# Nine tokens on a partition: a new layout of q, k, V and of the result in a threshold-attention and maxout kernel

## The chip, the cores and the metric

The kernel runs on one core of a Trainium2 chip. Time is device time in microseconds (us) of one execution. An execution that is over 1.5% above the fastest of the same kernel counts as slow. Ratios leave these out; the medians quoted include them. Engines: PE multiplies matrices, DVE reduces and does elementwise work, ACT evaluates activations, POOL does elementwise work, and SP's queue issues transfers. Sixteen DMA engines carry the transfers.

Ratios are the mean time of one kernel's fast runs over that of the other's fast runs of the same rounds, with a 95% interval, so they are not quite the ratio of the medians quoted beside them.

## The reference

Attention over 8 batches of 8 heads, 576 tokens and head size 64, in which only scores within tau of the row's maximum count, followed by a feed-forward layer that takes the maximum of three products:

```python
scores = scale * q @ k^T
scores = where(scores >= max(scores) - tau, scores, -1e9)
attn = softmax(scores)
x = (attn @ v), heads side by side        # 4608 x 512
h = max(x @ w1, x @ w2, x @ w3)           # 4608 x 768
out = h @ w_out                           # 4608 x 512
```

## The kernel before

Four heads of a batch make a "quad". A quad has nine steps of 128 queries for two heads; beside each step PE does two pieces of other work: transposes of the next quad's q and k (`tp`), products of the probabilities with V (`o`), hidden pieces of the feed-forward (`ph`), blocks of its output (`po`). In the profile's lines `sc` are scores, `P` the probabilities, `ptq` the transposed probabilities, and `ob` a block of the result that ACT copies out of PSUM and a store takes away. All PSUM results share four buffers. The probabilities are transposed by the DMA engines (`ptq<-P`), issued from the same SP queue as the loads and stores. The parts that the change touches, cut:

```python
# load: four tokens on a partition, the last 64 tokens apart
nc.sync.dma_start(out=L[n + "m"][:, hh],
                  in_=src[b, hs, 0:512, :].rearrange("h (p c) d -> p h c d", c=4))
nc.sync.dma_start(out=L[n + "r"][:, hh], in_=src[b, hs, 512:S, :].rearrange("h p d -> p h d"))
...
# transposed: four full transposes and a half one, five a head pair and tensor
for src in (m[:, h1, 0:2], m[:, h1, 2:4], r[:, h0:h0 + 2], m[:, h0, 0:2], m[:, h0, 2:4]):
    np_ = src.shape[0]
    tensor.transpose(ps[:, col:col + np_], src.rearrange("p a d -> p (a d)"), identf[:np_, :np_])
...
# product: the fifth block of keys has 64 rows
rows = slice(0, 64) if i == 1 else slice(64, 128)
w = vrb[rows, pr, :]
x = pt[rows, 4, q0:q0 + n]
...
# outp: 128 rows of the result, or the last 64
rows = out[b * S:b * S + 512, :].rearrange("(p c) m -> c p m", c=4)[c] if c < 4 \
    else out[b * S + 512:(b + 1) * S, :]
nc.sync.dma_start(out=rows, in_=ob[:r])
```

Of the kernel before, what the change touches and what calls it, by code (L numbers as in the profile page):

```python
# [11 lines left out]
F32 = mybir.dt.float32  # L12
# [34 lines left out]
def kernel(  # L47
# [19 lines left out]

    nc = tc.nc
# [30 lines left out]
    qk = ctx.enter_context(tc.tile_pool(name="qk", bufs=4))  # L99
# [12 lines left out]
    def load(b, qd, split=False):  # L112
        h = slice(4 * qd, 4 * qd + 4)
        L = dict(b=b, qd=qd)
        for n in "qk":
            L[n + "m"] = ld.tile([128, 4, 4, D], F32, name=n + "m")
            L[n + "r"] = ld.tile([64, 4, D], F32, name=n + "r")
        for hh in ((slice(0, 2), slice(2, 4)) if split else (slice(0, 4),)):
            for n, src in (("q", q), ("k", k)):
                hs = slice(4 * qd + hh.start, 4 * qd + hh.stop)  # L120
                nc.sync.dma_start(out=L[n + "m"][:, hh],
                                  in_=src[b, hs, 0:512, :].rearrange("h (p c) d -> p h c d", c=4))
                nc.sync.dma_start(out=L[n + "r"][:, hh], in_=src[b, hs, 512:S, :].rearrange("h p d -> p h d"))
        vm = ld.tile([128, 4, 4, D], F32, name="vm")
        vr = ld.tile([128, 2, D], F32, name="vr")
        nc.sync.dma_start(out=vm, in_=v[b, h, 0:512, :].rearrange("h (p c) d -> p h c d", c=4))
        rest = v[b, h, 512:S, :].rearrange("(t i) p d -> i p t d", i=2)
        nc.sync.dma_start(out=vr[0:64], in_=rest[1])
        nc.sync.dma_start(out=vr[64:128], in_=rest[0])
        L["vm"], L["vr"] = vm, vr  # L130
        return L

    def cast_v(L):
        vb = vp.tile([128, 4, 4, D], BF16, name="vb")
        vrb = vp.tile([128, 2, D], BF16, name="vrb")
        pool.tensor_copy(out=vb, in_=L["vm"])
        pool.tensor_copy(out=vrb, in_=L["vr"])
        L["vb"], L["vrb"] = vb, vrb

    def transposed(L, n, pr):  # L140

        m, r = L[n + "m"], L[n + "r"]
        ps = slot("tp")
        h0, h1 = 2 * pr, 2 * pr + 1
        col = 192
        for src in (m[:, h1, 0:2], m[:, h1, 2:4], r[:, h0:h0 + 2], m[:, h0, 0:2], m[:, h0, 2:4]):
            np_ = src.shape[0]
            tensor.transpose(ps[:, col:col + np_], src.rearrange("p a d -> p (a d)"), identf[:np_, :np_])
            col += np_
        t = qk.tile([128, S], F32, name=n + "t")  # L150
        if n == "q":
            scalar.activation(out=t, in_=ps[:, 192:768], func=AF.Copy, scale=scale)
            s = qk.tile([128, S], F32, name="qs")
            pool.tensor_copy(out=s[0:64], in_=t[64:128])
            pool.tensor_copy(out=s[64:128], in_=t[0:64])
            L["qs", pr] = s
        else:
            vector.tensor_copy(out=t, in_=ps[:, 192:768])
        L[n + "t", pr] = t


    def scores(L, idx, i):

        ps = slot("sc")
        first = 256 if i == 1 else 192
        for r in range(2):
            cols = slice(first, 512) if r == 0 else slice(512, first + S)
            if i == 1:
                kc = slice(0, 256) if r == 0 else slice(0, 320)
            else:  # L170
                kc = slice(256, 576) if r == 0 else slice(320, 576)
# [14 lines left out]
    def masked(idx, i):  # L186
        return i == 0 and idx in MASKED

    def maximum(idx, i, sc):
# [3 lines left out]
        if masked(idx, i):  # L193
            return nm
# [251 lines left out]
```

## Time and profile before

| | before |
|---|---|
| time, median | 542.63 us (541.65 to 543.3) |
| steady stage, one batch | 62.45 us, PE busy 61.2, DVE 50.9, ACT 50.3 |
| score pieces, first start | 9.43 us |
| time of SP's packets, as a share of the span of 16 DMA engines | 72.9% |

The prediction shows the page's main rows. Two more matter in hindsight: the transfers' totals, and the profile's account of the transposing transfers (durations of the issue in ns, lowest, median and highest; then the time from issue to landing).

```profile
DMA packets 220086, 84.06 MB, mean 156 GB/s; under 512 B 185472, under 2 KB 215424, under 8 KB 220032
q1 hardware_dynamic: 214464, 80.24, 72.9%
...
L224 SPq DMA_TRANSPOSE ptq<-P x144: 1242/1308/7147, 18.9 to 512.5; - x144
...
DMA to landing us min/median/max: 3.2/3.5/15.3
```

The packets of SP's queue take nearly three quarters of what 16 engines have, without being what bounds the kernel: DMA is 3% of the end-setting chain. A transposing transfer is issued in 1.3 us and lands after 3.5. The 72.9% is a mean over 16 engines: it leaves room if the work stays spread evenly over them.

### The profile page before, as it was taken

How to read it: one execution, taken by the hardware profiler on the slowest of the kernel's cores; microseconds unless marked ns; L12 is line 12 of the kernel's file. 1: busy time of each engine (PE TensorE's matmuls, PEld its weight loads, DVE VectorE, ACT ScalarE, POOL GpSimd, SP SyncE). 2: the span in 40 equal slices, each digit the busy share in tenths (PEclk: the TensorE clock that was granted, in tenths of full speed). 3: DMA queues.
4: the chain of work that ended last, by engine and by line, in shares of the span. 5: the costliest groups of instructions: out<-in, count | busy, mean ns of one | idle time of the engine just before them, and what ended most of it. 6: DMA issues, size and time to landing. Idle time of an engine off the chain costs nothing.

```text
span 537.3 us, 10760 instructions
## 1 busy us (share of the span) xinstructions
PE 502.1 (93%) x3638; PEld 305.5 (57%) x3652; DVE 412.4 (77%) x988; ACT 405.0 (75%) x819; POOL 292.1 (54%) x402
## 2 busy tenths in 40 slices
PE   7779759999999999999999999999999999899996
PEld 4335336565566645665566655666566665566563
DVE  2998956887598868887699867888688896587542
ACT  3998966687877878788787878878877878686732
POOL 3688984554554745565465545647455665342310
PEclk9999887999999999999999999999999999899999
DMA  7999999996976678879866587966879446543461
GB/s 212 234 240 199 207 154 180 222 189 140 201 177 126 144 190 138 178 127 190 188 154 130 127 208 167 191 130 147 191 135 173 89 90 143 100 88 70 132 106 49
DMA packets 220086, 84.06 MB, mean 156 GB/s; under 512 B 185472, under 2 KB 215424, under 8 KB 220032
## 3 DMA queue, kind: packets, MB, share of 16 engines
q1 hardware_dynamic: 214464, 80.24, 72.9%
q0 software_dynamic: 5568, 3.15, 5.0%
q8 instruction: 28, 0.46, 0.4%
q14 instruction: 26, 0.21, 0.1%
HBM read 34.60 MB, written 9.44 MB: 82 GB/s over the span
## 4 chain that ended last, share of the span: by engine, by line
PE 68%; DVE 13%; ACT 4%; DMA 3%; issue 1%; POOL 0%; ACTq 0%; DVEq 0%
PE sc L35 23%; PE ph L35 22%; PE po L35 9%; PE o L35 8%; DVE nm L35 6%; PE tp L35 6%; DMA ptq<-P 3%; ACT z L35 3%; DVE hm L35 2%; DVE z L35 1%; DVE hT L35 1%; DVE bm L35 1%; ACT xt L35 1%; ACT hm L35 0%; DVE xt L35 0%
## 5 line engine op out<-in xcount | busy, mean ns | idle before, releaser
L35 POOL TENSOR_SCALAR P<-z,rs 128x576 bf16<-128x576 f32 x288 | 214.1, 756 | 209.8 <-ACT z L35 179.3
L35 DVE TENSOR_REDUCE nm<-sc 128x1 f32<-128x576 f32 x288 | 215.8, 750 | 54.1 <-PE sc L35 54.0
L35 ACT ACTIVATE z<-sc,bm 128x576 f32<-128x576 f32 x192 | 141.9, 741 | 87.6 <-DVE bm L35 66.0
L35 PE MATMUL sc<-kt,qs 64*128 64x320 f32 (+2 forms) x640 | 186.9, 435 | 6.7 <-ACT z L35 6.0
L35 PE MATMUL sc<-kt,qt 64*128 64x256 f32 (+2 forms) x640 | 185.5, 445 | 3.6 <-ACT z L35 3.5
L35 PE MATMUL ph<-xt,w 128*128 128x288 bf16 (+2 forms) x1152 | 157.2, 289 | 3.4 <-ACT xt L35 2.6
L35 PEld LDWEIGHTS <-w 128*128 128x128 bf16 x1152 | 107.3, 98 | 55.9 <-issue 28.9
L35 ACT ACTIVATE z<-z 128x576 f32<-128x576 f32 x192 | 130.4, 683 | 0.0
L35 PEld LDWEIGHTS sc<-kt,qs 64*128 64x128 f32 (+1 forms) x640 | 91.6, 178 | 40.5 <-ACT z L35 28.1
L35 PEld LDWEIGHTS sc<-kt,qt 64*128 64x128 f32 (+1 forms) x640 | 92.2, 178 | 25.0 <-ACT z L35 10.3
L35 DVE SCALAR_TENSOR_TENSOR z<-z 128x576 f32<-128x576 f32 x96 | 76.0, 792 | 0.0
L35 ACT ACTIVATE z<-sc,nm 128x576 f32<-128x576 f32 x96 | 70.9, 739 | 0.0
L35 PE MATMUL po<-wo,hT 128*128 128x512 bf16 (+1 forms) x226 | 56.4, 381 | 2.2 <-DVE hT L35 1.5
L35 POOL COPY qs<-qt 64x576 f32<-64x576 f32 x64 | 48.9, 764 | 9.6 <-ACT qt L35 6.2
L35 DVE TENSOR_TENSOR hm<-ph,hm 128x576 bf16<-128x576 f32 (+2 forms) x54 | 36.9, 682 | 22.4 <-PE ph L35 9.2
L35 PE MATMUL o<-ptq,vb 128*64 128x288 bf16 (+3 forms) x528 | 44.4, 290 | 8.8 <-DMA ptq<-P 6.5
L35 ACT ACTIVATE hm<-ph 128x576 bf16<-128x576 f32 (+2 forms) x54 | 32.2, 595 | 15.0 <-PE ph L35 14.3
L35 PEld LDWEIGHTS <-hT 128*128 128x128 bf16 (+1 forms) x240 | 22.2, 100 | 31.4 <-issue 7.0
L35 DVE TENSOR_TENSOR hT<-ph,hm 128x576 bf16<-128x576 f32 (+2 forms) x54 | 36.9, 683 | 3.8 <-PE ph L35 1.2
L35 PEld LDWEIGHTS <-vb 128*64 128x64 bf16 x528 | 24.4, 109 | 25.9 <-issue 15.6
L35 ACT ACTIVATION_READ_ACCUMULATOR z<-z 128x1 f32 x192 | 38.6, 201 | 0.0
L35 PE MATMUL tp<-identf,qm 128*128 128x128 f32 x128 | 28.9, 309 | 6.3 <-DMA qm<-in_q_dram 3.6
(28 smaller groups left out, 296.7 us busy)
## 6 DMA issues: line engine op xcount, KB each, us to landing
vm<-in_v_dram SPq DMA_DIRECT2D x16, 512.0 KB, 4.9
out_dram<-ob SPq DMA_DIRECT2D x32, 256.0 KB, 2.6
qm<-in_q_dram SPq DMA_DIRECT2D x15, 512.0 KB, 4.4
km<-in_k_dram SPq DMA_DIRECT2D x15, 512.0 KB, 5.0
ptq<-P SPq DMA_TRANSPOSE x144, 3.5
w<-in_moe_w_dram POOLq DMA_DIRECT2D x9, 256.0 KB, 9.1
vr<-in_v_dram SPq DMA_DIRECT2D x32, 32.0 KB, 4.1
out_dram<-ob SPq DMA_DIRECT2D x8, 128.0 KB, 2.8
```

Source lines behind the costliest of these rows:

```text
L35: ins = fn(*a, **kw)
```

## The change

The intent: with nine tokens of a head on each of 64 partitions, and two heads on 128, all transposes are full ones, runs in HBM grow to 2304 bytes, V's last keys need no 64-row matmuls, and the last tokens of the result use both halves of the array's columns. The core of the diff, cut:

```diff
+        def part(src, r, i=None):
+            h = slice(4 * qd + r, 4 * qd + 4, 2) if i is None else slice(4 * qd + r + 2 * i, 4 * qd + r + 2 * i + 1)
+            return src[b, h].rearrange("i (p c) d -> i p c d", c=9)
+
+        for i in ((0, 1) if first else (None,)):
+            rows = slice(0, 128) if i is None else slice(64 * i, 64 * i + 64)
+            q2 = nc.scalar if first else nc.sync
+            nc.sync.dma_start(out=L["q"][rows, 0:9], in_=part(q, 0, i))
+            q2.dma_start(out=L["k"][rows, 0:9], in_=part(k, 0, i))
 ...
+        nj = 5 - r
+        for j in range(nj):
+            tensor.transpose(ps[:, 128 * j:128 * j + 128], couple(L, n, r, j),
+                             identf)
 ...
+                for r in range(2):
+                    x = pt[:, 4 if m == 4 else m + 5 * r, q0:q0 + n]
 ...
+            rows = out[b * S:(b + 1) * S, :].rearrange("(p c) m -> c p m", c=9)
+            if c < 4:
 ...
+                rows = rows[first:first + 5:4]
 ...
+                    for x in range(2):
+                        tensor.matmul(ps[64 * x:64 * x + 64, :256], hT[:, f, 512:S], wo[:, f, 256 * x:256 * x + 256],
+                                      start=(f == 0), stop=(f == NF - 1))
 ...
+                rows = rows[8].rearrange("p (x m) -> x p m", x=2)
 ...
-    for a in prep:
-        transposed(Ls[0], *a)
+    for a in prep[:1] + prep[1:2]:
+        transposed_one(Ls[0], a[0], 0)
```

`transposed_one` does the first quad's transposes for one head pair at a time with 64 rows, so that the first scores need not wait for the other pair.

More of the change, by code (lines that the diff above doesn't have):

```diff
@@ L98 @@
     vp = ctx.enter_context(tc.tile_pool(name="vp", bufs=3))
-    qk = ctx.enter_context(tc.tile_pool(name="qk", bufs=4))
+    qk = ctx.enter_context(tc.tile_pool(name="qk", bufs=2))
     zz = ctx.enter_context(tc.tile_pool(name="zz", bufs=4))
@@ L109, in slot @@
         return ps_s.tile([128, 1024], F32, name=name, tag="s")
-    def load(b, qd, split=False):
-        h = slice(4 * qd, 4 * qd + 4)
-        L = dict(b=b, qd=qd)
-        for n in "qk":
-            L[n + "m"] = ld.tile([128, 4, 4, D], F32, name=n + "m")
-            L[n + "r"] = ld.tile([64, 4, D], F32, name=n + "r")
-        for hh in ((slice(0, 2), slice(2, 4)) if split else (slice(0, 4),)):
-            for n, src in (("q", q), ("k", k)):
-                hs = slice(4 * qd + hh.start, 4 * qd + hh.stop)
-                nc.sync.dma_start(out=L[n + "m"][:, hh],
-                                  in_=src[b, hs, 0:512, :].rearrange("h (p c) d -> p h c d", c=4))
-                nc.sync.dma_start(out=L[n + "r"][:, hh], in_=src[b, hs, 512:S, :].rearrange("h p d -> p h d"))
-        vm = ld.tile([128, 4, 4, D], F32, name="vm")
-        vr = ld.tile([128, 2, D], F32, name="vr")
-        nc.sync.dma_start(out=vm, in_=v[b, h, 0:512, :].rearrange("h (p c) d -> p h c d", c=4))
-        rest = v[b, h, 512:S, :].rearrange("(t i) p d -> i p t d", i=2)
-        nc.sync.dma_start(out=vr[0:64], in_=rest[1])
-        nc.sync.dma_start(out=vr[64:128], in_=rest[0])
-        L["vm"], L["vr"] = vm, vr
@@ new lines, with load @@
+    FIRST = dict(q=((0, 4, 2, 6), (10, 14, 12, 16)), k=((4, 0, 6, 2), (14, 10, 16, 12)))
+    vms = [one.tile([128, 4, 5, D], F32, name=f"vm{x}") for x in range(2)]
+    def load(g, first=False):
+        b, qd = quads[g]
+        L = dict(b=b, qd=qd, vm=vms[g % 2])
+        for n in "qk":
+            L[n] = ld.tile([128, 18, D], F32, name=n + "m")
+        def part(src, r, i=None):
[6 more added lines that the diff above has]
+            q2.dma_start(out=L["k"][rows, 0:9], in_=part(k, 0, i))
+            nc.sync.dma_start(out=L["q"][rows, 10:18], in_=part(q, 1, i)[:, :, 0:8])
+            nc.sync.dma_start(out=L["q"][rows, 9:10], in_=part(q, 1, i)[:, :, 8:9])
+            q2.dma_start(out=L["k"][rows, 9:18], in_=part(k, 1, i))
+        for r in range(2):
+            src = part(v, r).rearrange("i p c d -> p i c d")
+            for half, c0, c1, at_ in (((0, 4, 9, 0), (1, 0, 4, 0)), ((0, 5, 9, 1), (1, 0, 5, 0)))[r]:
+                nc.sync.dma_start(out=L["vm"][64 * half:64 * half + 64, 2 * r:2 * r + 2, at_:at_ + c1 - c0, :],
+                                  in_=src[:, :, c0:c1, :])
@@ L131, in load @@
         return L
     def cast_v(L):
-        vb = vp.tile([128, 4, 4, D], BF16, name="vb")
-        vrb = vp.tile([128, 2, D], BF16, name="vrb")
+        vb = vp.tile([128, 4, 5, D], BF16, name="vb")
         pool.tensor_copy(out=vb, in_=L["vm"])
-        pool.tensor_copy(out=vrb, in_=L["vr"])
-        L["vb"], L["vrb"] = vb, vrb
-    def transposed(L, n, pr):
-        m, r = L[n + "m"], L[n + "r"]
-        ps = slot("tp")
-        h0, h1 = 2 * pr, 2 * pr + 1
-        col = 192
-        for src in (m[:, h1, 0:2], m[:, h1, 2:4], r[:, h0:h0 + 2], m[:, h0, 0:2], m[:, h0, 2:4]):
-            np_ = src.shape[0]
-            tensor.transpose(ps[:, col:col + np_], src.rearrange("p a d -> p (a d)"), identf[:np_, :np_])
-            col += np_
-        t = qk.tile([128, S], F32, name=n + "t")
-        if n == "q":
-            scalar.activation(out=t, in_=ps[:, 192:768], func=AF.Copy, scale=scale)
-            s = qk.tile([128, S], F32, name="qs")
-            pool.tensor_copy(out=s[0:64], in_=t[64:128])
-            pool.tensor_copy(out=s[64:128], in_=t[0:64])
-            L["qs", pr] = s
-        else:
-            vector.tensor_copy(out=t, in_=ps[:, 192:768])
-        L[n + "t", pr] = t
@@ L162, in scores, with couple @@
-    def scores(L, idx, i):
-        ps = slot("sc")
-        first = 256 if i == 1 else 192
-        for r in range(2):
-            cols = slice(first, 512) if r == 0 else slice(512, first + S)
-            if i == 1:
-                kc = slice(0, 256) if r == 0 else slice(0, 320)
-            else:
-                kc = slice(256, 576) if r == 0 else slice(320, 576)
-            rows = slice(64 * r, 64 * r + 64)
+        L["vb"] = vb
+    def couple(L, n, r, j, rows=slice(0, 128)):
+        f = 8 if j == 4 else FIRST[n][r][j]
+        return L[n][rows, f:f + 2, :].rearrange("p a d -> p (a d)")
@@ new lines, in evacuated, with targets @@
+    def evacuated(L, n, dst, src):
+        if n == "q":
+            scalar.activation(out=dst(L["qt"]), in_=src, func=AF.Copy, scale=scale)
+            for x in range(2):
+                pool.tensor_copy(out=dst(L["qs"])[64 * x:64 * x + 64], in_=dst(L["qt"])[64 - 64 * x:128 - 64 * x])
+        else:
+            vector.tensor_copy(out=dst(L["kt"]), in_=src)
+    def targets(L, n):
+        if n + "t" not in L:
+            L[n + "t"] = qk.tile([128, 2, S], F32, name=n + "t")
+            if n == "q":
+                L["qs"] = qk.tile([128, 2, S], F32, name="qs")
@@ new lines, in transposed, with transposed_one @@
+    def transposed(L, n, r):
+        targets(L, n)
+        ps = slot("tp")
+        nj = 5 - r
+        for j in range(nj):
+            tensor.transpose(ps[:, 128 * j:128 * j + 128], couple(L, n, r, j),
+                             identf)
+        off = 320 * r
+        evacuated(L, n, lambda t: t[:, :, off:off + 64 * nj].rearrange("p i (j u) -> p i j u", u=64),
+                  ps[:, 0:128 * nj].rearrange("p (j i u) -> p i j u", i=2, u=64))
+    def transposed_one(L, n, i):
+        targets(L, n)
+        ps = slot("tp")
+        rows = slice(64 * i, 64 * i + 64)
+        col = 256
+        for r, j in [(0, j) for j in range(5)] + [(1, j) for j in range(4)]:
+            tensor.transpose(ps[:, col:col + 64], couple(L, n, r, j, rows),
+                             identf[rows, rows])
+            col += 64
+        evacuated(L, n, lambda t: t[:, i, :], ps[:, 256:256 + S])
@@ L173, in scores @@
+    def scores(L, idx, r):
+        ps = slot("sc")
+        first = 256 if r == 0 else 192
+        for x in (1, 0):
+            cols = slice(first, 512) if x == 1 else slice(512, first + S)
+            if r == 0:
+                kc = slice(0, 256) if x == 1 else slice(0, 320)
+            else:
+                kc = slice(256, 576) if x == 1 else slice(320, 576)
+            rows = slice(64 * x, 64 * x + 64)
             if idx != 4:
-                pr, c = (0, idx) if idx < 4 else (1, idx - 5)
@@ L175, in scores @@
-                t = L["qt", pr] if c % 2 == r else L["qs", pr]
-                off = (0 if i == 1 else 320) + 128 * (c // 2)
-                tensor.matmul(ps[:, cols], t[rows, off:off + 128], L["kt", pr][rows, kc],
+                i, c = (0, idx) if idx < 4 else (1, idx - 5)
+                t = L["qt"] if c // 2 == x else L["qs"]
+                off = 320 * r + 128 * (c % 2)
+                tensor.matmul(ps[:, cols], t[rows, i, off:off + 128], L["kt"][rows, i, kc],
                               start=True, stop=True)
@@ L179, in scores @@
             else:
-                for pr in range(2):
-                    t = L["qt", pr] if i == r else L["qs", pr]
-                    tensor.matmul(ps[64 * pr:64 * pr + 64, cols], t[rows, 256:320],
-                                  L["kt", pr][rows, kc], start=True, stop=True)
+                for i in range(2):
+                    t = L["qt"] if r == x else L["qs"]
+                    tensor.matmul(ps[64 * i:64 * i + 64, cols], t[rows, i, 256:320],
+                                  L["kt"][rows, i, kc], start=True, stop=True)
@@ L184, in scores, with masked, maximum @@
         return ps[:, first:first + S]
-    def masked(idx, i):
-        return i == 0 and idx in MASKED
-    def maximum(idx, i, sc):
+    def masked(idx, r):
+        return r == 1 and idx in MASKED
+    def maximum(idx, r, sc):
         nm = small.tile([128, 1], F32, name="nm")
         vector.tensor_reduce(out=nm, in_=sc, axis=AX, op=OP.max, negate=True)
-        if masked(idx, i):
+        if masked(idx, r):
             return nm
@@ L197, in maximum, with exponents @@
         return bm
-    def exponents(idx, i, z, sc, bias):
-        zn = z[:, (1 - i) * S:(2 - i) * S]
-        if masked(idx, i):
+    def exponents(idx, r, z, sc, bias):
+        zn = z[:, r * S:(r + 1) * S]
+        if masked(idx, r):
             scalar.activation(out=zn, in_=sc, func=AF.Exp, bias=bias)
@@ L205, in exponents, with numerators @@
             scalar.activation(out=zn, in_=sc, func=AF.Prelu, bias=bias, alpha=-STEEP)
-    def numerators(L, idx, i, z, sm):
-        n = 1 - i
-        zn = z[:, n * S:(n + 1) * S]
-        acc = sm[:, n:n + 1]
-        if masked(idx, i):
+    def numerators(L, idx, r, z, sm):
+        zn = z[:, r * S:(r + 1) * S]
+        acc = sm[:, r:r + 1]
+        if masked(idx, r):
             vector.scalar_tensor_tensor(out=zn, in0=zn, scalar=thr, in1=zn,
@@ L224, in normalized, with product @@
         nc.sync.dma_start_transpose(out=L["pt"][:, :, idx * 128:(idx + 1) * 128], in_=P)
-    def product(L, pr, xt, part=None):
+    def product(L, i, xt, part=None):
         ps = slot("o")
-        pt, vb, vrb = L["pt"], L["vb"], L["vrb"]
+        pt, vb = L["pt"], L["vb"]
         if part is None:
-            q0, p0 = (0, 224) if pr == 0 else (S, 192)
+            q0, p0 = (0, 224) if i == 0 else (S, 192)
             runs = ((q0, p0, 512 - p0), (q0 + 512 - p0, 512, S - 512 + p0))
         elif part == 1:
-            runs = ((0 if pr == 0 else S + 64, 0, 256),)
+            runs = ((0 if i == 0 else S + 64, 0, 256),)
         else:
-            runs = ((256, 0, 320),) if pr == 0 else ((S + 320, 0, 256), (S, 512, 64))
+            runs = ((256, 0, 320),) if i == 0 else ((S + 320, 0, 256), (S, 512, 64))
         for q0, p0, n in runs:
             for m in range(5):
-                for i in (1, 0):
-                    h = 2 * pr + i
-                    if m < 4:
-                        w = vb[:, h, (0, 2, 1, 3)[m], :]
-                        x = pt[:, (m if i == 1 else 5 + m), q0:q0 + n]
-                    else:
-                        rows = slice(0, 64) if i == 1 else slice(64, 128)
-                        w = vrb[rows, pr, :]
-                        x = pt[rows, 4, q0:q0 + n]
-                    tensor.matmul(ps[64 * i:64 * i + 64, p0:p0 + n], w, x, start=(m == 0), stop=(m == 4))
-        dst = xt[:, 2 * L["qd"] + pr, :]
-        if part is None and pr == 0:
+                for r in range(2):
+                    x = pt[:, 4 if m == 4 else m + 5 * r, q0:q0 + n]
+                    tensor.matmul(ps[64 * r:64 * r + 64, p0:p0 + n], vb[:, 2 * r + i, ((1, 3, 0, 2, 4), (2, 4, 1, 3, 0))[r][m], :], x,
+                                  start=(m == 0), stop=(m == 4))
+        dst = xt[:, 2 * L["qd"] + i, :]
+        if part is None and i == 0:
             vector.tensor_copy(out=dst, in_=ps[:, 224:224 + S])
@@ L257, in product @@
             scalar.activation(out=dst[:, 0:256], in_=ps[:, 0:256], func=AF.Copy)
-        elif pr == 0:
+        elif i == 0:
             vector.tensor_copy(out=dst[:, 256:S], in_=ps[:, 0:320])
@@ L288, in outp @@
         def outp(c):
-            r = 128 if c < 4 else 64
             ps = slot("po")
-            for f in range(NF):
-                tensor.matmul(ps[:r, :512], hT[:, f, c * 128:c * 128 + r], wo[:, f, :],
-                              start=(f == 0), stop=(f == NF - 1))
-            ob = hp_.tile([128, DM], F32, name="ob", bufs=3)
-            scalar.activation(out=ob[:r], in_=ps[:r, :512], func=AF.Copy)
-            rows = out[b * S:b * S + 512, :].rearrange("(p c) m -> c p m", c=4)[c] if c < 4 \
-                else out[b * S + 512:(b + 1) * S, :]
-            nc.sync.dma_start(out=rows, in_=ob[:r])
+            rows = out[b * S:(b + 1) * S, :].rearrange("(p c) m -> c p m", c=9)
+            if c < 4:
+                for f in range(NF):
+                    tensor.matmul(ps[:, :512], hT[:, f, c * 128:c * 128 + 128], wo[:, f, :],
+                                  start=(f == 0), stop=(f == NF - 1))
+                ob = hp_.tile([128, DM], F32, name="ob", bufs=3)
+                first = (0, 2, 1, 3)[c]
+                rows = rows[first:first + 5:4]
+                scalar.activation(out=ob, in_=ps[:, :512], func=AF.Copy)
+            else:
+                for f in range(NF):
+                    for x in range(2):
+                        tensor.matmul(ps[64 * x:64 * x + 64, :256], hT[:, f, 512:S], wo[:, f, 256 * x:256 * x + 256],
+                                      start=(f == 0), stop=(f == NF - 1))
+                ob = hp_.tile([128, DM // 2], F32, name="obr", bufs=2)
+                rows = rows[8].rearrange("p (x m) -> x p m", x=2)
+                scalar.activation(out=ob, in_=ps[:, :256], func=AF.Copy)
+            nc.sync.dma_start(out=rows, in_=ob)
         return ([lambda f=f, wi=wi: hid(f, wi) for f in range(NF) for wi in range(3)]
@@ L314, with o_step @@
     todo = []
-    def o_step(g, pr, part=None):
+    def o_step(g, i, part=None):
         b = quads[g][0]
@@ L319, in o_step @@
             xts[b] = xp.tile([128, 4, S], BF16, name="xt")
-        product(Ls[g], pr, xts[b], part)
-        if pr == 1 and quads[g][1] == 1:
+        product(Ls[g], i, xts[b], part)
+        if i == 1 and quads[g][1] == 1:
             if b not in hTs:
@@ L344 @@
         at(18 * g + 18 + (15 if early else 8), lambda g=g: o_step(g, 1))
+    at(0, lambda: transposed_one(Ls[0], "q", 1))
+    at(1, lambda: transposed_one(Ls[0], "k", 1))
     e = 18 * y
@@ L361 @@
     wl = list(weight_loads())
-    Ls[0] = load(*quads[0], split=True)
-    for a in prep:
-        transposed(Ls[0], *a)
-    sc = [scores(Ls[0], 0, 1), scores(Ls[0], 0, 0)]
+    for x in range(2):
+        for t in vms:
+            vector.memset(t[64 - 64 * x:128 - 64 * x, 2 * x:2 * x + 2, 4 - 4 * x, :], 0.0)
+    Ls[0] = load(0, first=True)
+    for a in prep[:1] + prep[1:2]:
+        transposed_one(Ls[0], a[0], 0)
+    sc = [scores(Ls[0], 0, 0), scores(Ls[0], 0, 1)]
     late, prev = None, []
@@ L372 @@
             nx = n // 9 + 1
-            Ls[nx] = load(*quads[nx])
+            Ls[nx] = load(nx)
         if n == 1:
@@ L379 @@
         sm = small.tile([128, 2], F32, name="sm")
-        cur = [(L, idx, i, z, sm) for i in (1, 0)]
-        bias = [maximum(idx, i, sc[1 - i]) for i in (1, 0)]
+        cur = [(L, idx, r, z, sm) for r in range(2)]
+        bias = [maximum(idx, r, sc[r]) for r in range(2)]
         for c in prev:
@@ L384 @@
                 numerators(*c)
-        for i in (1, 0):
-            exponents(idx, i, z, sc[1 - i], bias[1 - i])
+        for r in range(2):
+            exponents(idx, r, z, sc[r], bias[r])
         for c in prev:
@@ L397 @@
             g2, idx2 = steps[n + 1]
-            sc = [scores(Ls[g2], idx2, 1), scores(Ls[g2], idx2, 0)]
+            sc = [scores(Ls[g2], idx2, 0), scores(Ls[g2], idx2, 1)]
         if wl and n >= 14:
```

## The prediction

> **What bounds the kernel now.** I read the page's rows of busy engines and the 40 slices first, then a table of windows by stage, then the chain that ended last, and only then single instructions in time order.
>
> ```profile
> span 537.3 us, 10760 instructions
> PE 502.1 (93%) x3638; PEld 305.5 (57%) x3652; DVE 412.4 (77%) x988; ACT 405.0 (75%) x819; POOL 292.1 (54%) x402
> ...
> PE 68%; DVE 13%; ACT 4%; DMA 3%; issue 1%; POOL 0%; ACTq 0%; DVEq 0%
> ```
>
> PE leads, but the averages mix four stages. The table of windows (columns: busy us of each engine with its number of instructions, the granted clock, the DMA share, GB/s) separates them:
>
> ```profile
> 30.00:40.00 10.00, 6.89 (x48) 2.81 (x45) 9.76 (x27) 9.60 (x22) 7.94 (x11) 1.00 1.07 251
> 70.00:80.00 10.00, 4.34 (x31) 2.54 (x32) 5.24 (x14) 6.70 (x14) 8.75 (x12) 0.83 1.49 153
> 319.85:382.30 62.45, 61.22 (x452) 37.63 (x454) 50.89 (x123) 50.28 (x102) 35.17 (x48) 1.00 0.77 162
> 510.00:537.30 27.30, 22.88 (x169) 14.68 (x169) 10.01 (x23) 7.14 (x15) 2.47 (x4) 1.00 0.38 76
> ```
>
> Until about 66 us there is no feed-forward work yet and DVE (9.76 of 10) with ACT sets the pace. At 66 to 83 us the transposing transfers are late (DMA share 1.49; the chain holds one piece "DMA ptq<-P" of 13.53 us), PE sits idle and then runs at a reduced clock (0.65 in the window 80 to 90). From about 85 to 510 us PE is busy 98% of each batch of 62.45 us, that is, two quads of four heads plus one feed-forward. From 510 us on PE runs the last feed-forward alone. So most of the gain must come from PE time in the steady stage, 425 / 62.45 = 6.8 batches. But DVE is busy 50.9 of 62.45 us there, and unevenly.
>
> **What PE spends.** Time order of PE in one step of that stage (start, duration):
>
> ```profile
> 336.44 0.44 PE L35 MATMUL tp<-identf,qm 128*128 128x128 f32 x2
> 336.81 0.28 PE L35 MATMUL tp<-identf,qr 64*128 64x64 f32 x1
> 337.02 0.44 PE L35 MATMUL tp<-identf,qm 128*128 128x128 f32 x2
> 337.29 0.38 PE L35 MATMUL tp<-identf,km 128*128 128x128 f32 x2
> 337.61 0.27 PE L35 MATMUL tp<-identf,kr 64*128 64x64 f32 x1
> 337.81 0.44 PE L35 MATMUL tp<-identf,km 128*128 128x128 f32 x2
> 338.18 0.48 PE L35 MATMUL sc<-kt,qs 64*128 64x256 f32 x1
> ...
> 347.22 0.68 PE L35 MATMUL o<-ptq,vb 128*64 128x288 bf16 x8
> 347.83 0.31 PE L35 MATMUL o<-ptq,vrb 64*64 64x288 bf16 x2
> 348.07 0.68 PE L35 MATMUL o<-ptq,vb 128*64 128x288 bf16 x8
> 348.68 0.31 PE L35 MATMUL o<-ptq,vrb 64*64 64x288 bf16 x2
> 348.92 0.48 PE L35 MATMUL sc<-kt,qt 64*128 64x256 f32 x1
> ```
>
> The starts carry this reading, not the modelled durations. Transposes: two full ones and a change to 64 rows take 0.37 us (336.44 to 336.81), four full ones and a change take 0.59 (337.02 to 337.61), so a full transpose costs 0.11 us and a change of array shape 0.15. The half transposes with one change take 0.20, so 0.05 each. Ten cost 8 x 0.11 + 2 x 0.05 + 5 x 0.15 = 1.73 us, which is the chain's "PE tp L35 x10". Product out of V: eight matmuls (four column pairs side by side) and a change take 0.61, one half-row pair and a change 0.24; hence a pair costs 0.123 and a change 0.12. One product is 1.70 us, of which four changes.
>
> **What the Trainium skill says.** "TensorEngine Tiling (Array Packing)", Key Properties: "Changing tiling mode (not just tile) drains the TensorE". The trace agrees, and sizes it at 0.12 to 0.15 us here. "Perfetto Trace Analysis", Identifying the Most-Contended Engine, warns that matmul busy time is a poor measure of distance to the limit; the trace agrees, for PE's 98% contain these drains. "DMA: Bandwidth & Descriptors", Specifications, gives 512 B as the least transfer for line rate; the rest loads of this kernel are 256-byte runs. The trace agrees only in part: it counts small packets (185472 of 220086 are under 512 B), yet most belong to the transposing transfers, which this change leaves alone. The same page, Issuing engines are not separate DMA queues, says issuing from several engines only saves issue time; I use that for the first loads of k on ACT's queue.
>
> **The change, part by part.**
>
> 1. *Transposes.* A quad has 2 x 10 now (16 full, 4 half), later 18 full, in one step of ten (both tensors, first heads) and one of eight. New cost 10 x 0.11 + 0.15 = 1.25 and 8 x 0.11 + 0.15 = 1.03, against 2 x 1.73 = 3.46. PE saves 1.2 us a quad, 2.4 a batch. The evacuations move as many elements as before (640 + 512 against 2 x 576), so ACT, DVE and POOL save nothing.
>
> 2. *V padded to 128 keys.* The fifth key block needs no 64-row tile: ten pairs of one shape, 10 x 0.123 + 0.12 = 1.35 against 1.70. It saves 0.35 a product, four products a batch, 1.4 us. The cast of V (1038 + 296 ns) becomes one of 1280 columns, about 1.3 us: nothing changes on POOL.
>
> 3. *Output of ninth tokens.* Six matmuls of 512 columns on half the array (322.84 to 324.25, 1.41 us with the change of shape) become six pairs of 256 side by side, about half: 0.64 saved per batch. ACT's evacuation falls from 587 to some 380 ns.
>
> 4. *Loads.* Per quad, runs fall from 512 of 1 KB and 256 of 256 B per tensor (2304) to 384 for q, 256 for k and 512 for v (1152), with nine issues of 0.6 us rather than seven. From the load-heavy early windows (near 300 GB/s over 16 engines) a 1-KB run takes about 57 ns. Taking some 20 ns of that as fixed, my choice, a quad's loads fall from about 6.9 to 5.5 us of all DMA engines: 1.4 us, an estimate from these rates. This lies on the end-setting path only in the congested stretch, 49 to 83 us, where the weights (12 transfers of 256 KB) and the transposes dominate. There fall about 1.3 quads of loads: some 2 us off the 13.5 us wait.
>
> 5. *Start.* Now all 20 transposes precede the first scores (9.43 us). Afterwards only 64-row halves of the first head pair do (18 short ones), k's loads go out on ACT's queue beside q's, and the rest follows in steps 0 and 1. Counting 0.6 us an issue and landing 2.9 us later as today, scores start near 7.5. One DVE copy of 0.74 us moves behind it into a stage that DVE bounds, so I take 1.5 us.
>
> **What of the PE saving reaches the end.** PE saves 2.4 + 1.4 + 0.64 = 4.4 us a batch. But in time order DVE runs from 329.8 to 341.5 us, the stretch with both transpose steps and one step of two feed-forward pieces, without a real gap; the next scores after the first transposes already wait for ACT:
>
> ```profile
> 331.91 1.37 PE sc L35 x7
> 333.27 2.07 PE ph L35 x16
> 335.34 1.17 PE sc L35 x8
> 336.51 1.73 PE tp L35 x10
> 338.25 1.17 PE sc L35 x8
> ```
>
> An undisturbed piece is 1.17; here 1.37, 0.2 of waiting. At the second transposes the score buffers came free only 0.2 to 0.3 us before PE needed them. So a faster transpose step mostly lets PE wait: I count 0.4 of its 2.4 us. The products and the ninth tokens lie where DVE waits for PE (gaps of 0.9 to 2.2 us around 322 to 330, 1.2 around 376 and 380, 1.5 at 360), so they count almost fully: 1.4 + 0.64. That is about 2.4 a batch, times 6.8 = 16 us. The tail (last two products, one output block) gives 1 us. **Sum: 16 + 2 + 1.5 + 1 = 20.5 us, so 521.5 us.**
>
> **Rivals.**
> - *Everything on PE counts.* For it: PE at 98% in the steady stage, 68% of the chain. Against it: DVE's unbroken run beside the transposes. It would give 6.8 x 4.4 + 4.5 = 34 us: 508.
> - *DVE with ACT takes over wholly.* DVE needs 50.9 us plus hand-overs per batch, and score, maximum, exponent, free buffer is a loop through three engines and four buffers. Then only some 1.2 us a batch come through: 8 + 4 = 12 us: 530. Against it: DVE sits idle up to 2.2 us at a time waiting for PE where products and outputs stand.
> - *The loads give nothing, or cost.* Two more issues a quad sit in the same queue as the transposing transfers, whose late landing stops PE at 75 to 80 us; if the weights alone cause that, the stretch stays and the clock drop behind it too: 2 to 4 us less gain. For the reverse: a shorter backlog also saves the idle PE and its low clock, up to 5 us more.
>
> **Range and chances.** Centre 521.5. The two outer accounts give 508 and 530; the early stretch adds 3 either way. I take 510 to 532. Faster by over 2% means below 531.2: 0.86. Within 2%: 0.13. Slower: 0.01, as no part adds work on a bounding engine.
>
> **What would show it.** In the changed trace: steps of ten and eight full transposes of 1.2 and 1.0 us in PE's time order, followed by score pieces that wait for ACT; products of 1.35 us without 64-row pieces; the ninth tokens in some 0.7 us; a batch near 60 us, with PE busy down to 57 and DVE still 51, now 85% of it; first scores before 8 us; the DMA wait at 66 us down to 11 or so. It is wrong if the batch shrinks by over 4 us (transposes counted after all), by under 1 us (the three-engine loop binds everywhere), or if the early stall grows or vanishes.

## The result, and the profile after

The changed kernel takes 894.14 us (889.95 to 895.58) against 542.63: a ratio of 1.6468 (1.6401 to 1.6535). The prediction of 521.5 us, and its range to 532, were wrong by far. The page of the changed kernel, in the rows that answer to those of before:

```profile
span 893.6 us, 10855 instructions
PE 530.2 (59%) x3686; PEld 331.7 (37%) x3686; DVE 414.8 (46%) x992; ACT 403.2 (45%) x819; POOL 288.3 (32%) x386
...
DMA packets 201085, 84.07 MB, mean 94 GB/s; under 512 B 174150, under 2 KB 188742, under 8 KB 201030
q1 hardware_dynamic: 195142, 79.65, 73.1%
...
DMA 31%; SPq 22%; PE 21%; DVE 15%; ACT 4%; POOL 3%; issue 2%; POOLq 0%; ACTq 0%; DVEq 0%
```

No engine of the core has grown much busier: DVE, ACT and POOL are busy as long as before, PE 28 us longer at a lower mean clock (0.78 against 0.984). The end-setting chain (the work that ended last, followed back) has moved from PE (68%) to transfers and to SP's queue (53% together). The bytes are the same, the packets fewer, and the rate has fallen from 156 to 94 GB/s. The mean share of the DMA engines is 73.1%, as good as unchanged; that row alone shows no saturation, and it counts time in which a packet only waits. The waits (who waited for whom: us in total, times, longest) and the transposing transfers say where it hurts:

```profile
PE o L35 <- DMA ptq<-P: 173.4, 29, 20.0
POOL P L35 <- DMA ptq<-P: 147.2, 19, 14.6
...
ACT ob L35 <- DMA out_dram<-ob: 115.0, 7, 24.9
...
L257 SPq DMA_TRANSPOSE ptq<-P x144: 1243/2232/16951, 55.0 to 858.3; - x144
```

Products wait for transposed probabilities, ACT waits for stores, and one issue of a transpose takes up to 17 us where it took at most 7. In time order SP's queue shows what stands before them; lines 136, 137 and 138 are the loads of q and k for the second heads:

```profile
9.51 3.98 SPq L136 DMA_DIRECT2D qm<-in_q_dram  x1
13.54 5.60 SPq L137 DMA_DIRECT2D qm<-in_q_dram  x1
19.18 5.02 SPq L138 DMA_DIRECT2D km<-in_k_dram  x1
```

An issue that took 0.6 us before takes 4 to 5.6, even the 32-KB one on line 137: the queue is being held back by something slow ahead of it, at 10 to 25 us already, before the weights load.

The packet records of the trace name it. Counted per size: how many packets ran at the same time while at least one was under way, and their median duration.

```
                             before               after
2048 B (stores; after also q)  12.6 at a time, 84 ns   2.1 at a time, 84 ns
2304 B (q, k)                  -                       2.0 at a time, 93 ns
1280 B (v)                     -                       8.5 at a time, 55 ns
256 B (mostly transposes)      14.9 at a time, 18 ns   16.6 at a time, 18 ns
```

A long run is not slow in itself: 93 ns for 2304 B is better than the two runs of 1024 B (46 ns each) and one of 256 B (18 ns) that it replaces, 110 ns. But the loads of q and k and the stores run two at a time: exactly two of the 2304-byte packets are under way for 251 of the 299 us in which any is. The records name no engine, so that it is two engines is read from this count. The count is not exact, for records can overlap (16.6 at a time on 16 engines).

The Trainium skill says why, on a page that the prediction cites for other things: "DMA: Bandwidth & Descriptors", Why a DMA increments its semaphore by 16 and not by 1, under "How many engines (k)". A transfer is spread over the largest number up to 16 that divides both sides' slowest dimension that is not 1. The source `src[b, h]` of the change leads with two heads, and the target `rows[first:first + 5:4]` of a store with two tokens, so that number is 2. V's loads lead with 64 tokens. The trace agrees for the narrow ones, at 2.0 and 2.1; V's loads should use 16 and run 8.5 at a time on average.

Now the time can be added up for each of the two engines, from packet counts and the durations above: 5760 of 2304 B x 93 ns / 2 = 268 us; 6016 of 2048 B x 84 / 2 = 253; 1024 half rows of 1024 B x 46 / 2 = 24; 1920 of 256 B x 18 / 2 = 17: together 562 us. To it comes the sixteenth that each engine has of the rest: 165888 transposing packets at their mean of 24.5 ns before, 254 us, some 26 for V and 27 for the weights. That makes about 869 us, an estimate, of a span of 893.6. The same sum for one batch of the steady stage is 48.8 (q, k) + 24.4 (stores) + 31.8 (transposes) + 3.2 (V) = 108 us; in the trace the last three batches from step 72 to step 126 take 107.9, 107.6 and 106.4 us, against 62.5 before. The theory at this point is that these two engines are the bound.

### The profile page after: what moved, and what is told of

It reads as the page before. It is cut to its first block, busy times and chain, and to the rows that moved or that the text cites. A ratio compares the mean times of both kernels' runs of the same rounds, so it can differ in the third digit from the quotient of the medians.

```text
span 893.6 us, 10855 instructions
## 1 busy us (share of the span) xinstructions
PE 530.2 (59%) x3686; PEld 331.7 (37%) x3686; DVE 414.8 (46%) x992; ACT 403.2 (45%) x819; POOL 288.3 (32%) x386
## 3 DMA queue, kind: packets, MB, share of 16 engines
q1 hardware_dynamic: 195142, 79.65, 73.1%
## 4 chain that ended last, share of the span: by engine, by line
DMA 31%; SPq 22%; PE 21%; DVE 15%; ACT 4%; POOL 3%; issue 2%; POOLq 0%; ACTq 0%; DVEq 0%
DMA ptq<-P 26%; SPq L257 15%; PE ph L35 8%; DVE nm L35 7%; PE sc L35 7%; PE o L35 4%; ACT z L35 3%; POOL P L35 3%; DMA out_dram<-ob 3%; SPq L138 2%; DMA qm<-in_q_dram 2%; PE po L35 2%; DVE hm L35 2%; DVE z L35 1%; SPq L137 1%
## 5 line engine op out<-in xcount | busy, mean ns | idle before, releaser
L35 PE MATMUL sc<-kt,qs 64*128 64x256 f32 (+2 forms) x640 | 206.4, 475 | 78.7 <-ACT ob L35 61.1
L35 PE MATMUL sc<-kt,qt 64*128 64x320 f32 (+2 forms) x640 | 208.3, 487 | 20.7 <-ACT z L35 20.6
L35 PE MATMUL o<-ptq,vb 128*64 128x288 bf16 (+3 forms) x660 | 69.3, 364 | 198.7 <-DMA ptq<-P 173.4
L35 PEld LDWEIGHTS sc<-kt,qs 64*128 64x128 f32 (+1 forms) x640 | 100.9, 197 | 114.5 <-ACT ob L35 61.9
L35 PEld LDWEIGHTS <-vb 128*64 128x64 bf16 x660 | 43.3, 137 | 227.4 <-issue 156.5
L35 DVE CAST xt<-o 128x64 bf16<-128x64 f32 (+2 forms) x32 | 15.1, 471 | 204.2 <-PE o L35 204.2
L35 ACT ACTIVATE ob<-po 128x512 f32<-128x512 f32 x32 | 19.0, 597 | 122.3 <-DMA out_dram<-ob 115.0
L35 ACT ACTIVATE xt<-o 128x512 bf16<-128x512 f32 (+1 forms) x20 | 10.7, 534 | 135.8 <-DVE xt L35 117.8
L35 POOL COPY qs<-qt 64x640 f32<-64x640 f32 (+2 forms) x64 | 48.3, 755 | 14.7 <-ACT qt L35 11.5
L35 DVE TENSOR_TENSOR hm<-ph,hm 128x576 bf16<-128x576 f32 (+2 forms) x54 | 36.9, 683 | 21.6 <-ACT hm L35 12.9
L35 PE MATMUL tp<-identf,qm 128*128 128x128 f32 (+1 forms) x153 | 26.6, 309 | 32.8 <-ACT z L35 22.9
```

The lines of the kernel that those rows point to most:

```text
L35: ins = fn(*a, **kw)
```

## The experiments

Three theories stood. A: two engines carry q, k and the stores, and are the bound. B: long runs, or the step over every second head in HBM, are slow. C: more issues in SP's queue hold up the transposing transfers.

**e1, e2, e3: widen one group of transfers, the other, both.** Nothing but the cut of the transfers differs; sizes of runs, bytes and places stay.

```diff
# e1: each load of q and k per head: 64 partitions, leading with 64 tokens
-        for i in ((0, 1) if first else (None,)):
+        for i in (0, 1):
# e2: each store per token (or half row): 64 rows
-            nc.sync.dma_start(out=rows, in_=ob)
+            for x in range(2):
+                nc.sync.dma_start(out=rows[x], in_=ob[64 * x:64 * x + 64])
```

> The changed kernel, with each load of q and k cut into two, one per head of the pair (64 partitions each), so that the slowest dimension of its source is 64 tokens and not 2 heads; the run lengths, bytes and targets stay, 14 issues a quad in place of 9. Theory A (a transfer whose source or target leads with a dimension of 2 runs on only two of the 16 DMA engines): packets of 2304 bytes then run many at a time and not 2.0 at a time; the two engines keep only the narrow stores, 172 us of their own plus some 350 us as their sixteenth of the rest, so about 525 to 620 us in all. Theory B (long runs of 2304 bytes are slow in themselves, or the parity stride in HBM is): unchanged, 880 to 900 us. Theory C (more issues in the sync queue hold up the transposing transfers): slower than 894 us.

> The changed kernel with only each store of the result cut into two (64 rows, or 64 half rows, each), loads as in the change. Theory A: the loads of q and k still sit on two engines, 389 us of packets on each plus some 325 us of its share of the rest: 715 to 830 us. Theories B and C: within 2% of 894 us, C rather slower.

> The changed kernel with both cuts. Theory A: no transfer of q, k or the result is confined to two engines; what is left is what the prediction worked out, so 510 to 532 us, around 521. Theory B: 880 us or more. Theory C: the slowest of all, with 5 more issues a quad for loads and 5 more a batch for stores.

Measured: e1 638.77 us (ratio to before 1.1803), e2 790.65 us (1.461), e3 539.19 us (537.92 to 542.49; 0.9981, 0.9923 to 1.0039). In e1 the packets of 2304 B ran 8.8 at a time, in e3 9.5, with those of 2048 B at 10.2. That long runs are slow falls, for the runs are the same. The other half of B, the step over every second head, isn't tried here, for each cut transfer reads one head; e5 below keeps that step and takes 534.21 us, so it falls there. C falls as the main cause, for e3 issues the most and is by far the fastest of the three. A stands. Its size for e1 was missed: 638.8 against 525 to 620. A sum of packets leaves waits out; in e1 ACT still waits 26.5 us for stores. In e3 the rate, the issue of the transposes and ACT's waits are back near the kernel before:

```profile
DMA packets 204536, 84.10 MB, mean 157 GB/s; under 512 B 177600, under 2 KB 192192, under 8 KB 204480
...
L257 SPq DMA_TRANSPOSE ptq<-P x144: 1242/1334/4737, 21.7 to 512.4; - x144
...
ACT ob L35 <- DMA out_dram<-ob: 7.7, 2, 4.6
```

But e3 is not the predicted 521 either. It is level with the kernel before, and that had to be explained too.

**e4, e12: the same narrowing in the kernel before.** If A is right, the old kernel must suffer from stores that lead with 2, and less from ones that lead with 4. Both write rows to the wrong places on purpose.

```diff
-            rows = out[b * S:b * S + 512, :].rearrange("(p c) m -> c p m", c=4)[c] if c < 4 \
-                else out[b * S + 512:(b + 1) * S, :]
+            rows = out[b * S:(b + 1) * S, :].rearrange("(p c) m -> c p m", c=9)
+            rows = rows[c:c + 5:4] if c < 4 else rows[8]                                          # e4
+            rows = rows[c % 2:8:2, 32 * (c // 2):32 * (c // 2) + 32] if c < 4 else rows[8]       # e12
```

> The kernel before, with only its stores of 128 rows made to lead with a dimension of 2 (rows c and c+4 of each nine, as in the change; the result is wrong on purpose, in the order of its rows). Same run of 2048 bytes, same number of transfers. Theory A: each of two engines gets 2048 packets of 84 ns, 172 us, on top of some 390 us of its share of the rest, so the kernel becomes bound by these two: 560 to 640 us. Theories B and C: unchanged, 540 to 546 us.

> The kernel before, with its stores of 128 rows leading with a dimension of 4 (four tokens by 32 groups; wrong in the order of the rows on purpose). If the leading dimension sets the number of engines: the 2048-byte packets run about 4 at a time (2.4 with two, 12.6 before), each of four engines gets 1024 packets of 84 ns, 86 us, on top of some 390 us of its share of the rest, 476 us, which is under the span: 540 to 560 us. If any store in several pieces is slow whatever its leading dimension: about 608 us, as with two.

Measured: e4 608.18 us (1.1238), with 2.4 packets of 2048 B at a time; e12 571.77 us (1.0525), with 4.1. In the waits of e4, the first of these lines has no counterpart in the kernel before; the second stands there with 6.5 us:

```profile
ACT ob L35 <- DMA out_dram<-ob: 37.1, 14, 5.9
...
PE o L35 <- DMA ptq<-P: 32.5, 8, 13.9
```

So the leading dimension of the stores alone, with nothing else of the change, costs 12%, and the number at a time follows it: 2.4 with 2, 4.1 with 4, 12.6 with 128. The time of e12 was expected lower (540 to 560): by the sum four engines with 476 us of packets each are not full, and yet the time grew by 5%. That transfers come in bursts and hold others up for a while would explain it; no run isolates that.

**e5, e6: fewer issues, more result buffers.** e3 needs 14 load issues a quad. e5, with the stores cut as in e3, is wide with 9: tokens lead, the two heads alternate on the partitions, and the copy out of PSUM takes every second column. e6 adds result buffers.

```diff
-            return src[b, h].rearrange("i (p c) d -> i p c d", c=9)
+            return src[b, h].rearrange("i (p c) d -> p i c d" if i is None else "i (p c) d -> i p c d", c=9)
-                  ps[:, 0:128 * nj].rearrange("p (j i u) -> p i j u", i=2, u=64))
+                  ps[:, 0:128 * nj].rearrange("p (j u i) -> p i j u", i=2, u=64))
# e6 besides
-                ob = hp_.tile([128, DM], F32, name="ob", bufs=3)
+                ob = hp_.tile([128, DM], F32, name="ob", bufs=5)
```

> The changed kernel with the stores cut in two and the loads of q and k made wide in another way: tokens lead and the two heads alternate on the partitions, so one transfer of 128 partitions does for both heads, and the copy out of PSUM takes every second column. 9 load issues a quad as in the change, where the kernel with both cuts has 14. Theory D (with the narrow transfers gone, what holds the early stretch back, 3.5 us later at the first feed-forward piece than the kernel before, is the number of issues in the sync queue): 530 to 536 us. Theory E (it is the weights and the transposing transfers alone, or the later start): 537 to 541 us, as with both cuts. If copying every second column is slow, the DVE copy of 640 columns rises above 807 ns and the time above 541.

> As the run before, with 5 buffers for the result blocks in place of 3. The trace of the kernel with both cuts has ACT waiting for stores to land once a batch (chain near 380 us) and a stall at 134 to 144 us. If these waits cost time on the path: 2 to 6 us less than with 3 buffers; if they only moved ACT's idle time: the same within 1 us.

Measured: e5 534.21 us (0.9893, 0.9843 to 0.9943); e6 530.99 us (0.9838, 0.9792 to 0.9885). Both fall in their ranges, e5 in that of theory D, but the intervals of e3 (0.9923 to 1.0039) and e5 overlap, so that the number of issues costs something is likely and not shown. ACT's wait for stores (7.7 us in two pieces in e3, a PE clock of 0.50 at 144 to 147 us after one of them, 5.4 us in e5) is gone from e6's trace, which is 3 us faster than e5 in the same rounds.

**e7, e8: single parts of the change in the kernel before.** e7 pads V (three standing tiles with zeros, two small casts), e8 tiles the output of the last 64 tokens.

```diff
# e7
-                        rows = slice(0, 64) if i == 1 else slice(64, 128)
-                        w = vrb[rows, pr, :]
-                        x = pt[rows, 4, q0:q0 + n]
+                        w = vrb[:, i, pr, :]
+                        x = pt[:, 4, q0:q0 + n]
# e8, for c == 4
+                for f in range(NF):
+                    for x in range(2):
+                        tensor.matmul(ps[64 * x:64 * x + 64, :256], hT[:, f, 512:S], wo[:, f, 256 * x:256 * x + 256],
+                                      start=(f == 0), stop=(f == NF - 1))
```

> The kernel before with only V's fifth key block padded with zeros to 128 keys, loads as they were, two small casts on POOL in place of one. The prediction's step: 0.35 us a product, 32 products, nearly all of it counted: 9 to 11 us less (531 to 534). If DVE with ACT bounds those steps too: at most 4 us less.

> The kernel before with only the output of its last 64 tokens of a batch tiled over two column halves. The prediction's step: 0.64 us a batch, 8 batches, counted fully: 4 to 6 us less (537 to 539). If hidden: within 1.5 us of the kernel before.

Measured: e7 529.48 us (0.9825, 0.9763 to 0.9886), so padding V alone gives much of what the whole layout can. e8 539.95 us (1.0003, 0.9951 to 1.0054): no change in the time. What e8 gains and where it loses it shows in the starts of the maxima (DVE's first reduction of a step's scores), read step by step from the traces; here is how much later (+) or earlier (-) than in the kernel before a step's first maximum starts:

```
step   before at   e3     e5     e6     e7     e8     e9     e10    e11
   0     10.9     +0.3   +0.2   +0.3   +0.1   +0.3   -0.3   -0.0   +0.6
   2     14.6     +2.8   +2.7   +2.8   +0.1   +0.7   +0.1   +2.5   +1.0
  24     71.4     +4.5   +3.4   +3.7   +1.7   +1.9   +1.4   +4.2  +12.9
  28     92.2     +2.9   +2.0   +1.6   -5.4   +3.8   -5.7   +4.9   +5.5
  54    184.8     +4.5   +1.3   -1.4   -6.5   +3.2   -7.8   +2.6   +2.4
 126    435.8     -2.4   -5.6   -8.3  -10.7   +1.3  -14.7   -3.7   -4.5
```

Each column is one execution. e8 differs from the kernel before in nothing until its first output block, and yet it is 3.8 us late at step 28: that stretch, where weights and transposing transfers queue together, scatters by some us from run to run. The mean of e8's six runs shows no gain either, so where the steady stage's gain goes is not settled. From step 54 to 126, four batches of the steady stage, e8 gains 1.9 us, 0.48 a batch; e7 gains 4.2, 1.05 a batch; e3, e5, e6 and e9 all gain 6.9, which is 1.73 a batch; in the windows of single batches, 60.72 us instead of 62.45.

**e9, e10, e11: the start, the transposes, the weights.** All build on e6. The table shows that the change's start loses 2.5 us in the first two steps. e9 loads and transposes the first quad as every other; e11 issues the weights earlier besides. e10 puts one useless 64-row transpose into each group, to bring back the changes of array shape.

```diff
# e9
-    Ls[0] = load(0, first=True)
-    for a in prep[:1] + prep[1:2]:
-        transposed_one(Ls[0], a[0], 0)
+    Ls[0] = load(0)
+    for a in prep:
+        transposed(Ls[0], *a)
# e10 (not e9)
+            if j == 1:
+                tensor.transpose(ps[:, 960:1024], couple(L, n, r, j, slice(0, 64)), identf[0:64, 0:64])
# e11: e9, and
-        if wl and n >= 14:
+        if wl and n >= 8:
```

> The kernel with interleaved loads, split stores and 5 result buffers, with the change's special start undone: the first quad is loaded and transposed as every other (128 partitions, all 36 matmuls of transposing before the first scores), with k on the sync queue. In the traces the change's start reaches its first maximum 0.3 us later than the kernel before and then loses 2.5 us in the first two steps. If that start is what costs: 2 to 4 us less than with it (527 to 529). If it only shifts a wait of the DMA-bound stretch behind it: the same within 1 us.

> The kernel with interleaved loads, split stores and 5 result buffers, with one useless half transpose of 64 rows into a free column range inside each group of transposes, which puts back two changes of array shape each: 0.05 + 2 x 0.15 = 0.35 us of PE a group, 1.4 us a quad, 22 us over the kernel. If transposing hides behind DVE and ACT, as the prediction had it (0.4 of 2.4 us counted): 0 to 5 us more (531 to 536). If PE time counts there as elsewhere: 18 to 22 us more (549 to 553).

> As the plain start, with the weight transfers issued from step 8 instead of 14. If the stall near 66 to 84 us comes from weights and transposing transfers queueing together: 2 to 6 us less than the plain start; if the DMA engines are saturated there whatever the order: within 1.5 us, or worse.

Measured: e9 528.05 us (522.22 to 531.78; 0.9755, 0.9694 to 0.9815), e10 531.9 us (0.9859, 0.9802 to 0.9916), e11 530.28 us (0.9782, 0.9721 to 0.9844). e9 has the lowest ratio, though not clear of e6, e7 and e11, and beats both kernels: it is the changed kernel with wide transfers, five result buffers and the plain start. Its step 0 comes 0.6 us before that of e6, and it does not lose the 2.5 us after it. e10 costs within its scatter nothing, though PE does 22 us more by the sizes of the prediction: a batch takes 60.87 us instead of the 60.73 of e6, 0.14 more where PE got 2.8 more, so transposing is hidden. e11 shows no gain: it moved the stall and did not remove it. The chain of its trace waits 31.06 us for transposed probabilities from 45 us on, and step 24 starts 12.9 us late.

The intervals of e5, e6, e7, e9, e10 and e11 lie wholly below 1.

The page of e9 for its end-setting chain, and its table of windows for a batch, show where the bound lies now:

```profile
PE 48%; DVE 26%; ACT 8%; DMA 5%; POOL 3%; issue 2%; ACTq 0%; DVEq 0%; SPq 0%; POOLq 0%
...
319.85:380.57 60.72, 58.33 (x459) 36.50 (x456) 50.78 (x123) 49.76 (x102) 35.12 (x46) 1.00 0.79 167
```

PE's part of the chain falls from 68 to 48%, DVE's rises from 13 to 26%.

## Why the prediction was wrong, point by point

**The step that failed is part 4, the loads,** in the words "a quad's loads fall from about 6.9 to 5.5 us of all DMA engines". It took for granted that a transfer uses all 16. By the measured durations a quad's q and k take 24.4 us of each of two engines; spread over all 16, the whole quad's loads would fall from 5.3 to 4.7 us, 0.6 and not 1.4, an estimate: a 1-KB run took 46 ns and a 256-byte one 18, so the fixed part is near 9 ns and not the 20 chosen. The stores were not looked at at all, since their rows stay 2048 bytes long; so "no part adds work on a bounding engine" was wrong too. In place of it the runs showed 2.0 packets at a time, two engines with some 870 us of packets each by the sum above, and the cure with exactly that undone: 894 us with both groups narrow, 790.65 with narrow loads only, 638.77 with narrow stores only, 539.19 with neither. The reverse, narrow stores in the old kernel, costs 12% (608.18 us). None of the rivals named it. The third came nearest, with transfers that cost, but it counted issues, which e3 refutes as the main cause.

How the crowding on two engines delays the transposing transfers is less sure. Their packets keep a median of 18 ns while the sum of all 256-byte packets doubles from 4374 to 8630 us. The doubling sits in few packets: 1.5% of them take over 60 ns and hold 5356 of the 8630 us. Packets of 256 B that start while one of 2048 or 2304 B is under way take 229 ns in the mean, the others 22.9; in e3 it is 26.0 and 23.7, and in e4, with nothing narrow but the stores, 153 and 24. That fits a transfer spread over 16 engines that waits for its share on the two busy ones; which engine each packet ran on is not recorded.

**With the transfers wide, the other steps can be judged** (e3, e5, e6, e9 against the kernel before):

- Sizes on PE: right. In e3 the products and the transposes, in PE's time order, are

```profile
336.62 0.66 PE L35 MATMUL tp<-identf,qm 128*128 128x128 f32 x4
337.12 0.60 PE L35 MATMUL tp<-identf,km 128*128 128x128 f32 x4
338.15 0.48 PE L35 MATMUL sc<-kt,qt 64*128 64x256 f32 x1 [0.44 <-ACT z L35]
...
347.33 1.42 PE L35 MATMUL o<-ptq,vb 128*64 128x288 bf16 x20
348.68 0.48 PE L35 MATMUL sc<-kt,qt 64*128 64x256 f32 x1
```

  A product runs from 347.33 to 348.68, 1.35 us as worked out. Eight transposes take 1.53 us up to the next scores, of which the last 0.44 is waiting for ACT: the waiting that the prediction named. Ninth tokens take 0.78 us in e6 (predicted "some 0.7"; its own sum, 1.41 less 0.64, gives 0.77) against 1.41.
- What of it reaches the end: the mechanism was right and the size too high. A batch gains 1.73 us, not 2.4. Padded V counts 1.05 (e7) of the 1.4 counted, the ninth tokens 0.48 (e8) of 0.64. The remaining 0.2 would be the transposes', where 0.4 was counted, and e10 shows that they hide. DVE is 26% of the chain of e9, so it may set the pace in some steps with products too; no run isolates that.
- The start: wrong in sign. "Scores start near 7.5" became 9.75 us in e3, because the last load of q's first part landed only at 6.7 us:

```profile
6.71 0.79 PE L35 MATMUL tp<-identf,qm 64*128 64x64 f32 x5 [1.78 <-DMA qm<-in_q_dram]
...
9.75 0.79 PE L35 MATMUL sc<-kt,qs 64*128 64x256 f32 x1 [1.29 <-POOL qs L35]
```

  That load's issue ended at 2.85 us in the trace, so it landed 3.9 us later, where 2.9 was counted. Issuing k from ACT's queue did save issue time, for the first loads of q and k are both issued at 0.74 us. The scores then waited for the swapped copy on POOL, and the other half of the transposes fell into steps 0 and 1: 2.8 us late at step 2, where 1.5 us of gain had been counted. e9 without that start is level with the kernel before there.
- The early stall: not shown to shrink. The chain's wait for transposed probabilities there was 13.53 us before, 17.18 in e3, 12.96 in e5, 11.37 in e6 and 21.77 in e9, and from step 24 to 28 e7 and e9 gained 7 us where e8 lost 2. So the 2 us counted for it can't be told from chance.
- The sum for a repaired change: 521.5 us predicted, 539.19 with wide transfers alone, 528.05 with interleaved loads, the plain start and five result buffers as well. That this lies in the predicted range does not bear the prediction out, for it needed these repairs, and steps of the sum came out smaller.

## What to carry to other kernels

When a layout changes, read the slowest dimension of both sides of every transfer, not only its run length and bytes: here a leading 2 put it on what counts as two of sixteen DMA engines, and the mean busy share did not show it (72.9% and 73.1%). Count how many packets of a size run at a time. And when a change bundles several ideas, try each alone: padding V, one small edit, gave 1.05 of the 1.73 us a batch that the whole layout gave once it was mended, and in time the two can't be told apart (0.9825, 0.9763 to 0.9886, against 0.9755, 0.9694 to 0.9815).

## What the Trainium skill lacked or had wrong

- "DMA: Bandwidth & Descriptors", Rules for kernel authors, says of two transfers to disjoint partition halves not to bother and to use one of 128 partitions. Here cutting the loads in two halves of 64 partitions (e1) took 894 us to 639, because one transfer of 128 led with 2. The row "Use all 16 engines" of the same table states the condition; the two rows should point at each other.
- The same page gives no price for a whole kernel. In the runs a leading dimension of 2 in the stores alone cost 12% (e4) and one of 4 cost 5% (e12), with 2.4 and 4.1 packets at a time where 12.6 ran before. Nor does it say that other transfers issued from the same queue suffer: the longest issue of a transposing transfer went from 7.1 to 17.0 us.
- "TensorEngine Tiling (Array Packing)", Key Properties, says that a change of tiling mode drains PE and gives no time. Here it is 0.12 us between 128 and 64 rows in bf16 products and 0.15 us around fp32 transposes, both worked out in the prediction from starts in the trace, and 1.05 us a batch were gained when four products lost three changes each (e7).
